# Attention with normalised q and k, then a gated MLP: tokens regrouped from 4 on 112 partitions to 7 on 128, tails packed, and the order of every engine taken from a written plan

## The chip, the cores and the metric

The kernel runs on one core of one Trainium2 chip. The metric is device time in microseconds (us) of one execution; of the kernel before, three runs were timed. TensorE is called PE in the profile (its weight loads PEld), VectorE DVE, ScalarE ACT, GpSimd POOL, SyncE SP. Each engine works through its own list of instructions in order; DMA transfers are issued from the lists of SP, POOL and ACT and land later.

## The reference

Eight batches, 12 heads, 448 tokens, head size 64, all float32. First attention on RMS-normalised q and k, then a gated MLP on the joined heads (768 columns).

```python
q_n, k_n = rmsnorm(q, g_q), rmsnorm(k, g_k)          # x / sqrt(mean(x*x) + 1e-6) * g
scores = matmul(q_n, k_n^T) / 8
attn = exp(scores - max);  attn = attn / (sum(attn) + 1e-9)
x = matmul(attn, v), heads joined                     # (8, 448, 768)
h = relu(x @ w_in);  u, w = h[:, :512], h[:, 512:]
w_n = (w - mean(w)) / sqrt(var(w) + 1e-6)             # over the 512 columns
w_s = w_spatial @ w_n + b_spatial                     # mixes the 448 tokens
out = (u * w_s) @ w_out                               # (8, 448, 768)
```

## The kernel before, in words

**Tiling.** A token index is 4p + c, with p on 112 partitions and c from 0 to 3. So keys come in four tiles of 112, q and k tiles are 112x1024 for a group of four heads, and every product whose rows are tokens uses 112 columns of the array. The 24 groups G (8 batches b times 3) hold heads g, g+3, g+6, g+9 of a batch.

**Attention of a group.** Loads of q and k on SP's queue (L76), squares on POOL (L167), sums of squares on DVE (L173), Ln and Exp on ACT for the reciprocal root (L180, L181), scaling to bf16 on POOL (L189). Both tensors are then transposed, for groups 5 to 23 by a DMA on SP's queue (L211) with a scaling of k on DVE (L222), for groups 0 to 4 on PE (L200) with two evictions on DVE (L205, L206). Four steps n follow: each has four score matmuls with 64 rows (L234, two at a time in the two halves of the array) into four PSUM banks, and one ACT exp over all four banks (L244, 112x1792; in the first 12 steps two exps of 112x896). The next group's steps carry `sums` (L266, 16 matmuls with a ones tile of 32 columns, four at a time beside each other), `recip` (L274, L275: Ln and Exp on ACT), `values` (twice 16 matmuls, L285) and `xt_store` (L293, DVE).

**MLP of a batch.** `unit_v` (L311: four token tiles, six matmuls of 512 columns each), relu, `stats` (L317, L318), `ln_rstd` (L325, L326), `ln_apply` (L331, DVE); `unit_u` (L340: four times six matmuls of 448); `unit_s` (L350: the spatial product, four times four of 448, the bias as a 113th row; its gate L353 on DVE); `unit_o` (L364: eight times four of 384; evictions L367 on ACT or L369 on DVE) and the output DMA on SP (L371, L373).

**Order.** The loop over t (four steps a group) writes the order of all engines by hand. Step t computes scores and exps of its group, the sums or values of the group before, and one slice of the MLP of the batch that lies 15 steps back: the first `unit_v` comes at t = 15, after group 3 has all its scores. The last batch's MLP follows the loop. POOL's queue issues v (L80, one DMA a batch), w_in (L135), w_spatial (L140), w_out (L143) and the bias (L144, onto 17 partitions); at t = 15 DVE casts the bias into w_spT (L507), ahead of everything else that DVE has to do there, and DVE copies four transposed tiles of w_spatial after it (L149, L153).

**PSUM.** Four banks hold scores (one tile `pss` of four banks from step 12 on, two of two banks before), four rotate among all other products.

Of the kernel before, what the change touches and what calls it, by code (L numbers as in the profile page):

```python
# [14 lines left out]
PSUM = bass.MemoryType.PSUM  # L15


@with_exitstack
def kernel(
# [13 lines left out]
    nc = tc.nc  # L33
# [3 lines left out]
    P = 112  # L37
    NC = 4
    NG = 3
    scale = 1.0 / math.sqrt(D)  # L40

    pe, act, dve, pool, sync = nc.tensor, nc.scalar, nc.vector, nc.gpsimd, nc.sync

    ctx.enter_context(tc.manual_schedule())

    const = ctx.enter_context(tc.tile_pool(name="const", bufs=1))
    early_pools = ctx.enter_context(ExitStack())
    first = ctx.enter_context(tc.tile_pool(name="first", bufs=1))
    early_qt = ctx.enter_context(tc.tile_pool(name="early_qt", bufs=2))
    ps_e = early_pools.enter_context(tc.tile_pool(name="ps_e", bufs=2, space=PSUM, side="right"))  # L50
    ps_w = ctx.enter_context(tc.tile_pool(name="ps_w", bufs=4, space=PSUM))
    qk_pool = ctx.enter_context(tc.tile_pool(name="qk", bufs=4))
    sq_pool = ctx.enter_context(tc.tile_pool(name="sq", bufs=2))
    qn_pool = ctx.enter_context(tc.tile_pool(name="qn", bufs=2))
    qt_pool = ctx.enter_context(tc.tile_pool(name="qt", bufs=3))
    st_pool = ctx.enter_context(tc.tile_pool(name="st", bufs=4))
    v_pool = ctx.enter_context(tc.tile_pool(name="vp", bufs=2))
    e_pool = ctx.enter_context(tc.tile_pool(name="ep", bufs=4))
    r_pool = ctx.enter_context(tc.tile_pool(name="rp", bufs=2))
    x_pool = ctx.enter_context(tc.tile_pool(name="xp", bufs=2))  # L60
    m_pool = ctx.enter_context(tc.tile_pool(name="mp", bufs=1))
    o_pool = ctx.enter_context(tc.tile_pool(name="op", bufs=3))


    q_g = [q[b].rearrange("(l g) (p c) d -> g p l (c d)", g=NG, c=NC) for b in range(B)]
    k_g = [k[b].rearrange("(l g) (p c) d -> g p l (c d)", g=NG, c=NC) for b in range(B)]
    raw, vb = {}, {}

    def load(G, i, l0=0, nl=4):
        b, g = divmod(G, NG)  # L70
        if nl == 4:
            t = qk_pool.tile([P, 4, NC * D], FP, name="qf" if i == 0 else "kf")
        else:
            t = first.tile([P, 2, NC * D], FP, name=f"f{i}{l0}")
        raw[G, i, l0] = t
        sync.dma_start(out=t, in_=(q_g, k_g)[i][b][g][:, l0:l0 + nl])  # L76

    def load_v(b):
        t = v_pool.tile([P, H, NC, D], BF, name="vt")
        pool.dma_start(  # L80
            out=t.rearrange("p h c d -> p h (c d)"),
            in_=v[b].rearrange("h (p c) d -> p h (c d)", c=NC))
        vb[b] = t

    g_row = const.tile([1, 2, 2, D], FP)
# [3 lines left out]
    for l in (0, 2):  # L89
        load(0, 0, l, 2)  # L90
        load(0, 1, l, 2)
    for G in (1, 2, 3):
        load(G, 0)
        load(G, 1)


    eps = const.tile([128, 1], FP)
    dve.memset(eps, 1e-6)
    one_f = const.tile([1, 1], FP)
    dve.memset(one_f, 1.0)  # L100
    ones = const.tile([P, 32], BF)
    dve.memset(ones, 1.0)
    ident = const.tile([128, 128], BF)
    make_identity(nc, ident)


    w_in_u = const.tile([128, 6, DH], BF)
    w_in_v = const.tile([128, 6, DH], BF)
    w_out = const.tile([128, 4, DM], BF)
    w_spT = const.tile([113, NC, NC, P], BF)  # L110
    w_sp = const.tile([P, NC, S], BF)
    bst = const.tile([113, S], FP)
    vn_t = [const.tile([113, NC, DH], BF, name=f"vn{i}") for i in range(2)]
    for t in vn_t:
        pool.memset(t[96:113, :, :], 1.0)

    ps_d = ps_w.tile([128, 512], FP, name="ps")

    def dummies(n):
        for _ in range(n):  # L120
            pe.matmul(out=ps_d[:, 0:128], lhsT=ident, rhs=ident, start=True, stop=True)

    dummies(50)
    g2_row = const.tile([1, 128], FP)
    g2_col = const.tile([128, 1], FP)
    dve.scalar_tensor_tensor(out=g2_row, in0=g_row[:, 0].rearrange("o t d -> o (t d)"), scalar=scale,
                             in1=g_row[:, 1].rearrange("o t d -> o (t d)"),
                             op0=ALU.mult, op1=ALU.mult)
    ps_g = ps_w.tile([128, 512], FP, name="ps")
    pe.matmul(out=ps_g[:, 0:1], lhsT=g2_row, rhs=one_f, start=True, stop=True)  # L130

    def load_w_in(h):
        w = w_in_v if h else w_in_u
        for l in range(4):
            pool.dma_start(  # L135
                out=w[32 * l:32 * l + 32, :, :],
                in_=moe_w_in[192 * l:192 * l + 192, DH * h:DH * h + DH].rearrange("(j p) f -> p j f", p=32))

    def load_w_sp():
        pool.dma_start(out=w_sp, in_=moe_w_spatial.rearrange("(p c) s -> p c s", c=NC))  # L140

    def load_w_out():
        pool.dma_start(out=w_out, in_=moe_w_out.rearrange("(c p) m -> p c m", p=128))  # L143
        pool.dma_start(out=bst[96:113, :], in_=moe_b_spatial.partition_broadcast(17))  # L144

    def w_sp_unit(sc):
        ps = ps_w.tile([128, 8, 128], BF, name="ps")
        for t in range(NC):
            pe.matmul(out=ps[0:P, t, 0:P],  # L149
                      lhsT=w_sp[:, t, :].rearrange("p (s c) -> p c s", c=NC)[:, sc, :],  # L150
                      rhs=ident[0:P, 0:P], is_transpose=True,
                      start=(t == 0), stop=(t == NC - 1))
        dve.tensor_copy(out=w_spT[0:P, sc, :, :], in_=ps[0:P, 0:NC, 0:P])  # L153


    sqt, sqs, rst, nrm, qkt = {}, {}, {}, {}, {}

    def squares(G, i, l0=0, nl=4, eng=None):
        if nl == 4:
            t = sq_pool.tile([P, 4, NC * D], FP, name="sqt")  # L160
        else:
            t = first.tile([P, nl, NC * D], FP, name=f"s{i}{l0}")
        x = raw[G, i, l0]
        if eng is act:
            act.activation(out=t, in_=x, func=AF.Square, bias=0.0, scale=1.0)
        else:
            (eng or pool).tensor_tensor(out=t, in0=x, in1=x, op=ALU.mult)  # L167
        sqt[G, i, l0] = t

    def reduce(G, i, l0=0, nl=4):  # L170
        if (G, l0) not in sqs:
            sqs[G, l0] = st_pool.tile([P, 2, 4 * nl], FP, name="ms")
        dve.tensor_reduce(out=sqs[G, l0][:, i, :],  # L173
                          in_=sqt.pop((G, i, l0)).rearrange("p l (c d) -> p (l c) d", d=D),
                          axis=AX.X, op=ALU.add)

    def rstd(G, l0=0, nl=4):
        ln = st_pool.tile([P, 2, 4 * nl], FP, name="lnms")
        rst[G, l0] = st_pool.tile([P, 2, 4 * nl], FP, name="rs")
        act.activation(out=ln, in_=sqs[G, l0], func=AF.Ln, bias=eps[0:P, :], scale=1.0 / D)  # L180
        act.activation(out=rst[G, l0], in_=ln, func=AF.Exp, bias=0.0, scale=-0.5)  # L181

    def scaled(G, i, l0=0, nl=4, eng=None):
        if nl == 4:
            t = qn_pool.tile([P, NC, nl, D], BF, name=f"n{i}")
        else:
            t = first.tile([P, NC, nl, D], BF, name=f"n{i}{l0}")
        nrm[G, i, l0] = t
        (eng or pool).tensor_tensor(  # L189
            out=t.rearrange("p c l d -> p l c d"),  # L190
            in0=raw[G, i, l0].rearrange("p l (c d) -> p l c d", d=D),
            in1=rst[G, l0][:, i, :].rearrange("p (l c) -> p l c", c=NC).to_broadcast([P, nl, NC, D]),
            op=ALU.mult)

    def transposes(G, pr):
        ps = ps_w.tile([128, 8, 128], BF, name="ps")
        for i in range(2):
            for c in range(NC):
                x = nrm[G, i, 2 * pr] if (G, i, 2) in nrm else nrm[G, i, 0][:, :, 2 * pr:2 * pr + 2, :]
                pe.matmul(out=ps[:, 4 * i + c, 0:P], lhsT=x[:, c, :, :],  # L200
                          rhs=ident[0:P, 0:P], is_transpose=True,
                          start=(i == 0 and c == 0), stop=(i == 1 and c == NC - 1))
        qT = early_qt.tile([128, NC, P], BF, name=f"qe{pr}")
        kT = early_qt.tile([128, NC, P], BF, name=f"ke{pr}")
        dve.tensor_copy(out=qT, in_=ps[:, 0:4, 0:P])  # L205
        dve.tensor_scalar(out=kT, in0=ps[:, 4:8, 0:P], scalar1=g2_col, scalar2=None, op0=ALU.mult)  # L206
# [404 lines left out]
```

## Time and profile before

| | |
|---|---|
| timed runs | 337.10, 337.59 (median), 338.27 us |
| profiled execution | span 335.8 us from first to last instruction (the profile shows no other time of it) |
| busy | PE 298.2, PEld 144.9, DVE 222.2, ACT 223.5, POOL 187.5 us |
| exps | 84 of 112x1792 at 1662 ns, 24 of 112x896 at 913 ns |
| PE's records | 2484 matmuls |
| DMA | 50.45 MB, mean 150 GB/s |
| granted PE clock | mean 0.937 |

A row of groups reads: line, engine, operation, output and inputs with shapes, count, then busy time and mean length of one, then the engine's idle time just ahead of these instructions and what ended it. A busy PE row runs to the modelled end of a matmul and so overlaps the next one: rates of PE are read from start to start. In the table of windows, PEclk is the granted clock as a share of the full one.

### The profile page before, as it was taken

What the parts mean: (1) busy time and instruction counts of PE and PEld (TensorE: products, weight loads), DVE (VectorE), ACT (ScalarE), POOL (GpSimd) and SP (SyncE); (2) the same over time, 40 slices, a digit from 0 to 9 for tenths busy, and PEclk for the clock granted to TensorE, in tenths of its full rate; (3) what the DMA queues carried; (4) which work ended last, traced back from release to release, by engine and by line L of the source; (5) the groups of instructions that cost most, each with busy time, mean ns of one, the idle gap of its engine ahead of it and who ended that gap; (6) DMA issues with size and microseconds to landing.
All of it is one profiled execution on the core that took longest, in us unless ns stands there. A gap on an engine that the chain in (4) does not pass through costs nothing.

```text
span 335.8 us, 6167 instructions
## 1 busy us (share of the span) xinstructions
PE 298.2 (89%) x2484; PEld 144.9 (43%) x2484; DVE 222.2 (66%) x364; ACT 223.5 (67%) x275; POOL 187.5 (56%) x114
## 2 busy tenths in 40 slices
PE   6757674789999989998999899989998999999993
PEld 6432231434444435443454344434543354435552
DVE  3667754566964977497757877588658964735551
ACT  4648495047877687778687768777877877784331
POOL 5824699747468648665956774795487454000000
PEclk9678595659999999999999999999999999999999
DMA  7993969928458994799389966895679254002205
GB/s 187 241 238 73 187 148 208 207 37 154 111 133 206 190 212 86 206 203 238 68 209 191 183 155 193 174 208 145 171 191 197 49 129 119 27 2 82 84 0 167
DMA packets 75061, 50.45 MB, mean 150 GB/s; under 512 B 36911, under 2 KB 71440, under 8 KB 75032
## 3 DMA queue, kind: packets, MB, share of 16 engines
q1 hardware_dynamic: 61792, 41.76, 53.9%
q0 software_dynamic: 13232, 8.30, 17.9%
q8 instruction: 19, 0.31, 0.4%
q14 instruction: 10, 0.08, 0.1%
q10 hardware_dynamic: 8, 0.00, 0.0%
HBM read 38.58 MB, written 11.01 MB: 148 GB/s over the span
## 4 chain that ended last, share of the span: by engine, by line
POOL 33%; issue 28%; PE 22%; DVE 6%; DMA 6%; ACT 3%; ACTq 0%; POOLq 0%; DVEq 0%; SPq 0%
POOL sqt L167 19%; POOL n L189 11%; PE ps L311 4%; DMA bst<-in_moe_b_spatial_dram 4%; PE ps L364 3%; PE ps L340 3%; PE ps L285 2%; PE pss L234 2%; PE ps L266 2%; ACT et L244 2%; PE ps L350 2%; POOL vt L80 2%; DVE n L189 1%; PE pse L234 1%; PE ps L200 1%
## 5 line engine op out<-in xcount | busy, mean ns | idle before, releaser
L244 ACT ACTIVATE et<-pss 112x1792 bf16<-112x1792 f32 x84 | 139.6, 1662 | 58.4 <-PE pss L234 57.5
L189 POOL TENSOR_TENSOR n<-qf,rs 112x1024 bf16<-112x1024 f32 x22 | 45.9, 2086 | 88.2 <-ACT rs L181 76.4
L173 DVE TENSOR_REDUCE ms<-sqt 112x16 f32<-112x1024 f32 x46 | 55.6, 1215 | 45.2 <-POOL sqt L167 45.2
L364 PE MATMUL ps<-w_out,gt 128*112 128x384 bf16 x256 | 47.6, 330 | 2.9 <-DVE osb L369 2.6
L234 PE MATMUL pss<-qT,kT 64*112 64x448 bf16 x304 | 44.5, 369 | 5.8 <-ACT et L244 5.2
L311 PE MATMUL ps<-w_in_v,xt 128*112 128x512 bf16 x192 | 49.3, 404 | 0.0
L285 PE MATMUL ps<-et,vt 112*32 112x448 bf16 x768 | 46.1, 361 | 0.0
L167 POOL TENSOR_TENSOR sqt<-qf 112x1024 f32<-112x1024 f32 x22 | 42.6, 1934 | 0.0
L167 POOL TENSOR_TENSOR sqt<-kf 112x1024 f32<-112x1024 f32 x22 | 41.7, 1895 | 1.3 <-DMA kf<-in_k_dram 1.2
L340 PE MATMUL ps<-xt,w_in_u 128*128 128x448 bf16 x192 | 40.1, 354 | 0.0
L364 PEld LDWEIGHTS <-gt 128*112 128x112 bf16 x256 | 31.2, 129 | 19.9 <-issue 12.5
L293 DVE TENSOR_TENSOR xt<-ps,rc 128x448 bf16<-128x448 f32 x48 | 29.3, 615 | 15.5 <-PE ps L285 15.5
L189 POOL TENSOR_TENSOR n<-kf,rs 112x1024 bf16<-112x1024 f32 x19 | 38.8, 2040 | 0.0
L311 PEld LDWEIGHTS <-xt 128*112 128x112 bf16 x192 | 24.6, 137 | 21.1 <-issue 9.5
L369 DVE COPY osb<-ps 112x384 f32<-112x384 f32 x46 | 24.4, 552 | 7.6 <-PE ps L364 5.1
L234 PEld LDWEIGHTS <-kT 64*112 64x112 bf16 x304 | 14.9, 124 | 31.7 <-issue 31.4
L285 PEld LDWEIGHTS <-vt 112*32 112x32 bf16 x768 | 16.3, 97 | 25.4 <-issue 17.1
L350 PE MATMUL ps<-w_spT,vn 112*128 112x448 bf16 (+1 forms) x128 | 26.9, 353 | 0.0
L244 ACT ACTIVATE et<-pse 112x896 bf16<-112x896 f32 x24 | 20.5, 913 | 9.6 <-PE pse L234 9.5
L340 PEld LDWEIGHTS <-w_in_u 128*128 128x128 bf16 x192 | 17.1, 98 | 20.9 <-issue 7.2
L266 PE MATMUL ps<-et,ones 112*32 112x448 bf16 x384 | 24.8, 382 | 0.0
L317 DVE BATCH_NORM_STATS2 s<-vs 112x6 f32<-112x512 bf16 x32 | 21.7, 680 | 2.5 <-ACT vs L301 2.5
(59 smaller groups left out, 276.0 us busy)
## 6 DMA issues: line engine op xcount, KB each, us to landing
out_dram<-osb SPq DMA_DIRECT2D x31, 336.0 KB, 3.0
qf<-in_q_dram SPq DMA_DIRECT2D x23, 448.0 KB, 8.1
kf<-in_k_dram SPq DMA_DIRECT2D x23, 448.0 KB, 7.3
vt<-in_v_dram POOLq DMA_DIRECT2D x8, 672.0 KB, 13.1
w_in_v<-in_moe_w_in_dram POOLq DMA_DIRECT2D x4, 192.0 KB, 5.8
w_in_u<-in_moe_w_in_dram POOLq DMA_DIRECT2D x4, 192.0 KB, 8.0
w_out<-in_moe_w_out_dram POOLq DMA_DIRECT2D x1, 768.0 KB, 13.4
f<-in_q_dram SPq DMA_DIRECT2D x2, 224.0 KB, 4.0
```

The source lines that it names most:

```text
L167: (eng or pool).tensor_tensor(out=t, in0=x, in1=x, op=ALU.mult)
L173: dve.tensor_reduce(out=sqs[G, l0][:, i, :], in_=sqt.pop((G, i, l0)).rearrange("p l (c d) -> p (l c) d", d=D), axis=AX.X, op=ALU.add)
L189: (eng or pool).tensor_tensor(out=t.rearrange("p c l d -> p l c d"), in0=raw[G, i, l0].rearrange("p l (c d) -> p l c d", d=D), in1=rst[G, ...
L234: pe.matmul(out=ps[:, h, 0:S], lhsT=kT[64 * h:64 * h + 64, 2 * (n % 2) + c, :], rhs=qT[64 * h:64 * h + 64, :, :], start=True, stop=True)
L244: act.activation(out=exps[G, n // 2][:, c0:c0 + m, :], in_=ps[:, 0:m, 0:S], func=AF.Exp, bias=0.0, scale=1.0)
L266: pe.matmul(out=ps[32 * l:32 * l + 32, 0:S], lhsT=ones, rhs=exps[G, l // 2][:, 2 * c + l % 2, :], start=(c == 0), stop=(c == NC - 1), tile ...
L285: pe.matmul(out=ps[32 * l:32 * l + 32, 0:S], lhsT=vb[b][:, 3 * l + g, c, 32 * half:32 * half + 32], rhs=exps[G, l // 2][:, 2 * c + l % 2, ...
L293: dve.tensor_tensor(out=xts[b][:, 2 * g + half, :], in0=pst.pop((G, half))[:, 0:S], in1=rec[G], op=ALU.mult)
L311: pe.matmul(out=ps[0:P, :], lhsT=xts[b][:, j, c * P:(c + 1) * P], rhs=w_in_v[:, j, :], start=(j == 0), stop=(j == 5))
L340: pe.matmul(out=ps[:, 0:S], lhsT=w_in_u[:, j, 128 * f:128 * f + 128], rhs=xts[b][:, j, :], start=(j == 0), stop=(j == 5))
L350: pe.matmul(out=ps[:, 0:S], lhsT=vn_t[b % 2][0:kp, c, 128 * f:128 * f + 128], rhs=w_spT[0:kp, c, :, :].rearrange("p c s -> p (c s)"), star ...
L364: pe.matmul(out=ps[0:P, 0:384], lhsT=gts[b][:, f, c * P:(c + 1) * P], rhs=w_out[:, f, r], start=(f == 0), stop=(f == 3))
```

## The change

The kernel body is rewritten; the arithmetic of the reference stays. What differs:

- **Seven tokens a partition.** A token is 7p + c with p on 64 partitions, and two heads share the 128 partitions. A q or k tile of a group is 128x896 (rows of 1792 bytes), one DMA each.
- **128-key score tiles.** A head's keys are three tiles of 128 and a tail of 64. Twelve score matmuls of a group have 64 rows and 128 columns (units 0 to 5, two each); unit 6 is four matmuls of 64x64, two heads' tails beside each other in one bank. Each unit has one exp of 128x896: seven a group, 168 in all.
- **Sums and values** are passes of four matmuls (words s, a, b, four passes each); the tail pass uses ones and v with zeros on the other head's 64 rows (vz, zeroed once).
- **Transposes.** k of groups 1 to 23 and q of three of them go through PE (7 matmuls of 128 columns, word P, 26 times; group 0 in halves, word p) with one eviction of 128x896 (K: 22 on DVE, 4 on ACT); q of the other 20 groups goes by DMA (T).
- **MLP tiles.** Token tiles are three of 128 and a tail of 64. Word W puts the v product's tail of batch b (6 matmuls of 512, 64 columns at column 0 of the array) beside the output product's tail of batch b-1 (8 matmuls of 384, 64 columns at column 64). `ln_apply` moves to ACT (word A, Identity with scale and bias from tiles; one small DVE product w makes the bias).
- **Who does what.** Squares: 31 on POOL, 13 on ACT, 2 on DVE; scalings: 40 on POOL, 6 on DVE. v comes in four DMAs a batch on POOL's queue (32 in all, runs of 384 and 128 bytes); the bias comes in one row on SP's queue, its cast is a single row.
- **PSUM** is one tile of eight banks, each use with bank numbers from the plan; scores take any two banks, read as `ps[:, a:b+1:b-a, :]`.
- **Order.** The loop over t is gone. A string of 1649 words gives the order; a word's engine list is served in the order of the words. U and V come in three passes of two matmuls, sums and values in four, so that other work can stand between.

```diff
+PLAN = """
+l.1.0/0 setup//v l.0.0/1 l.1.1 l.0.1 L.1.0/2 L.1.1/3 L.2.1/4 gA//v L.4.0/5 gB/0 z.44/7 L.2.0/6 q.1.0/0/a r.1.0//v
...
+S.4.6/02 s.3.0/7 N.6.1/1/g E.4.6/d/a s.4.0/5 S.5.0/34 y.2//v s.4.1 L.10.1/2 I.7//a s.3.1 y.1//v s.4.2 J.7//a L.9.0/6
...
+SLOTS = dict(raw=7, sqt=3, nrm=4, qT=4, kr=0, kT=4, et=18, rc=2, vs=2, vn=2, us=2, os=4)
...
+    ps = psp.tile([128, 8, 512], FP, name="ps")
...
+    def op_wb(sl, e):
+        sync.dma_start(out=bst[64:65, :], in_=moe_b_spatial.rearrange("(o s) -> o s", o=1))
...
+    def op_P(sl, e, G, i):
+        where["tp", G, i] = sl[0]
+        p_ = ps[:, sl[0], :].bitcast(BF)
+        n = nrm[where.pop(("n", G, i))]
+        for m in range(C):
+            c = order[m] if i else m
+            pe.matmul(out=p_[:, 128 * m:128 * m + 128], lhsT=n[:, c, :, :], rhs=ident,
+                      is_transpose=True, start=(m == 0), stop=(m == C - 1))
...
+    def op_S(sl, e, G, u):
+        where["S", G, u] = sl
+        qT, kT = qTs[where["qk", G, 0]], kTs[where["qk", G, 1]]
+        if u == 6:
+            todo = [(r, hh, 6, T, 64 * hh, r) for hh in range(2) for r in range(2)]
+        else:
+            heads, j = unit(G, u)
+            todo = [(r, hh, 2 * j, 2 * T, 0, n) for n, (r, hh) in enumerate(heads)]
...
+            pe.matmul(out=ps[at:at + w, sl[n], 0:S],
+                      lhsT=kT[64 * r:64 * r + 64, hh, :, :].rearrange("q c p -> q (c p)")[:, 64 * c:64 * c + w],
+                      rhs=qT[64 * r:64 * r + 64, :, 64 * hh:64 * hh + 64],
+                      start=True, stop=True, tile_position=(64 * r, at))
+
+    def op_E(sl, e, G, u):
+        a, b = where.pop(("S", G, u))
+        where["et", G, u] = sl[0]
+        act.activation(out=ets[sl[0]], in_=ps[:, a:b + 1:b - a, 0:S], func=AF.Exp, bias=0.0, scale=1.0)
...
+    def op_W(sl, e, b):
...
+                todo.append((j / 6, dict(out=ps[0:64, sl[0], :], lhsT=xts[b % 2][:, j, TAIL:], rhs=w_in[:, j, DH:],
+                                         start=(j == 0), stop=(j == 5), tile_position=(0, 0))))
...
+                todo.append(((n + 0.5) / 8, dict(
+                    out=ps[64:128, sl[h - 2], 0:384], lhsT=gts[(b - 1) % 2][:, f, TAIL:],
+                    rhs=w_out[:, f, 384 * h:384 * h + 384], start=(f == 0), stop=(f == 3),
+                    tile_position=(0, 64))))
+        for _, args in sorted(todo, key=lambda x: x[0]):
+            pe.matmul(**args)
...
+    def op_A(sl, e, b, m):
...
+            act.activation(out=y, in_=x, func=AF.Identity, bias=nbs[b % 2][rows, m:m + 1], scale=rvs[b % 2][rows, m:m + 1])
...
+    for word in PLAN.split():
+        name, sl, e = (word.split("/") + ["", ""])[:3]
+        name, *args = name.split(".")
+        here["op_" + name]([int(x, 36) for x in sl], e, *map(int, args))
```

In a word such as `S.4.1/24` or `E.4.1/5/a` the part ahead of the first slash is the operation with its group (or batch) and unit, then come the banks or buffers, then the engine (a ACT, v DVE, g POOL).

## The prediction

> **What bounds the kernel now.** I read the page first, then the table of windows, then PE and the chain of waits inside the windows.
>
> ```profile
> span 335.8 us, 6167 instructions
> PE 298.2 (89%) x2484; PEld 144.9 (43%) x2484; DVE 222.2 (66%) x364; ACT 223.5 (67%) x275; POOL 187.5 (56%) x114
> PE   6757674789999989998999899989998999999993
> ACT  4648495047877687778687768777877877784331
> PEclk9678595659999999999999999999999999999999
> ```
>
> PE is the fullest engine, and its row has two parts: a quarter of the span at 5 to 7 tenths with the clock often near half, then 9 to the end. The windows put numbers to that:
>
> ```profile
> core 0: us, PE busy (x) PEld busy (x) DVE busy (x) ACT busy (x) POOL busy (x), PEclk, DMA share, GB/s
> 12.00:30.00 18.00, 13.80 (x114) 7.47 (x112) 11.41 (x12) 11.83 (x18) 6.73 (x4) 0.67 1.04 210
> 51.00:66.00 15.00, 9.38 (x48) 4.46 (x48) 7.63 (x8) 4.08 (x5) 13.57 (x10) 0.54 1.21 208
> 75.00:306.00 231.00, 222.62 (x1912) 103.39 (x1914) 165.18 (x276) 174.45 (x201) 139.71 (x76) 1.00 0.73 151
> ```
>
> From 75 on PE is busy 96% at the full clock; ACT and DVE have a quarter of the time free. That part is bound by PE. The start is not: ACT's rows in order of time show one hole, and the chain of waits says who made it.
>
> ```profile
> 69.58 1.66 ACT L244 ACTIVATE et<-pss 112x1792 bf16<-112x1792 f32 x1 [11.98 <-PE pss L234]
> ```
>
> ```profile
> 52.67 12.84 DMA bst<-in_moe_b_spatial_dram
> 65.53 0.56 DVE w_spT L507
> ...
> 68.54 0.99 PE pss L234 x4
> ```
>
> The bias, last in POOL's queue, lands after 12.84 us; the cast of it stands at the head of DVE's list, k's eviction is behind it, PE's scores wait for k, ACT for the scores. The first v product of the MLP (L311) starts at 71.7.
>
> **What a product costs on PE.** From PE's own rows, start to start:
>
> ```profile
> 289.18 0.94 PE L285 MATMUL ps<-et,vt 112*32 112x448 bf16 x16
> 290.05 1.31 PE L340 MATMUL ps<-xt,w_in_u 128*128 128x448 bf16 x6
> 291.29 0.58 PE L234 MATMUL pss<-qT,kT 64*112 64x448 bf16 x4
> 291.81 2.44 PE L340 MATMUL ps<-xt,w_in_u 128*128 128x448 bf16 x12
> 294.19 0.59 PE L234 MATMUL pss<-qT,kT 64*112 64x448 bf16 x4
> ```
>
> Twelve matmuls of 448 take 2.38 us, six 1.24: 0.19 each, and 0.10 that belongs to the run, not to a matmul. The 16 of L285 are four rounds of four beside each other: 0.87 = 4 x 0.19 + 0.11. The four of L234 are two rounds: 0.52 = 2 x 0.19 + 0.14. The same subtraction for L311 (x12 2.73, x6 1.43) gives 0.216 and 0.13, for L364 (x12 2.09, x8 1.44) 0.162 and 0.14. A run's fixed part comes at each change between score, 32-column and full-array matmuls; it is 0.13 to 0.14 where weights have 112 columns, 0.10 where 128, and weight loads differ too:
>
> ```profile
> L311 PEld LDWEIGHTS <-xt 128*112 128x112 bf16 x192 | 24.6, 137 | 21.1 <-issue 9.5
> L340 PEld LDWEIGHTS <-w_in_u 128*128 128x128 bf16 x192 | 17.1, 98 | 20.9 <-issue 7.2
> ```
>
> **PE, before and after, at the full clock.** Before: v products 192 x 0.216 = 41.5; u 192 x 0.189 = 36.3; spatial 128 x 0.189 = 24.2; output 256 x 0.162 = 41.5; scores 192 pairs x 0.189 = 36.3; sums and values (384 + 768)/4 x 0.189 = 54.4; transposes 5.4; 262 changes of shape x 0.125 = 32.8; dummies 4.3. Sum 276.7. After, counted in the plan's words: V 72 x 0.432 = 31.1; U 36.3; H 24.2; O 48 x 0.648 = 31.1; W about 12 (the two tails side by side: 6 x 0.216 = 1.30 beside 8 x 0.162 = 1.30; one after the other it would be 2.6); scores 168 rounds x 0.189 = 31.8; sums and values 288 x 0.189 = 54.4; 210 transposing matmuls of k and q 11 (0.053 each, from eight 128-column dummies in 0.85 us at the half clock); the w_spatial transposes about 1.5; 219 changes x 0.105 = 23.0; dummies 5.1. Sum 261.6, so **15 us less**: tails -8.7, score tiles -4.5, changes of shape -9.8, transposes +7. Bounds of what no row shows: W between 1.30 and 2.6 each (0 to +11 in all; I take side by side, as L285's four are); the 64x64 unit one or two rounds (0 to +4.5, likewise); k's moving rows in 64-column pieces as L234's 112-column pieces (0).
>
> The Trainium skill speaks against such interleaving: "TensorEngine Tiling (Array Packing)", section Tiling Modes, says that changing the tiling mode drains the array. The rows agree in kind, with their 0.10 to 0.14. By the rule alone a plan that cuts U and V in three and sums in four should lose; the counted changes fall, since sums and values of one or two groups stand together.
>
> **The other engines.** ACT: 168 exps x 913 = 153.4 (before 160.1); recip 27; Ln and Exp of the norms 12.7; `ln_apply` 32 x about 0.76 = 24 (nearest rows: the relu of 512 at 597, and Ln with a bias tile 312 against Exp without 229); squares 13 x 0.94 = 12.2; relus and output evictions 24.5; the rest 12. Sum about 266 against 223.5, so ACT becomes nearly as full as PE. But lengths overlap: two exps in a row take 1.72, not 1.83, and the rows at 16.55 (x4, 3.32) give 0.81 each, so in a row ACT needs about 230 to 235. DVE loses `ln_apply` (13.6) and 1/8 of L173's 55.6, gains evictions of 128x896 (about 0.82, as L222's 811): about 215, hidden at 70%. POOL falls from 187 to about 155 in spite of 32 v issues in place of 8 (w_in's issues of like size 0.58): hidden. SP: 20 transposes of 1.22 in place of 38, 56 output issues in place of 33: lighter. DMA: no more bytes, q and k rows of 1792 in place of 1024 bytes, half of the transposes gone, v in smaller runs: its share of 0.73 should not rise. Had any of these no cover, it is DVE that is next after ACT.
>
> Identity is in no row of before. The rows show Copy, Relu, Square, Ln and Exp under a single table load (L88, 1283 ns). If Identity needed its own table, A's 20 runs on ACT would cost 20 x 2 x 1.28 = 51; I take 0 by the five functions that share one load. "ScalarE: Activation LUTs", section "Table sets: the hidden batching unit", names identity among the cheap functions in every set; by it the cost is 0 as well, but no run here shows it yet.
>
> **The start.** The bias now comes on SP's queue and its cast stands after the first MLP products, so the hole of 12 goes. What is late next is ACT: the plan has 26 exps ahead of the first v product. First exp at about 12.5 (before 11.80; ACT's list ahead of it sums to 6.3). Then 26 x 0.81 to 0.913 = 21 to 24, and recip, norms, one square and one eviction 7.4: 41 with no wait. Loads by then: six groups 5.5 MB, w_in 3.1, v 1.4 = 10 MB; at the 208 GB/s of the rows above 48, but a part of w_in may land after. I take **46**, between 42 (no wait) and 57.6 (where before ended the exps of its 16th step, just ahead of the hole, so nothing gained but the hole).
>
> **The sum.** PE's list from the first v product on is 235.5, of which 34 after the last exp. At 95.6% busy (before: 33.6 of each 35.15 us of a batch) the first 201 take 210.6, the last at 98.5% 34.7. Span = 46 + 245.3 + 5.6 (before: last matmul at 330.2, end at 335.8: eviction, output DMA, landing) = 296.9. The median of the runs lies 1.8 over the profiled span: **299**.
>
> **The rivals.**
> - *Start not shortened beyond the hole* (loads bind): first v product at 57.6, all else the same: 310. For it: DMA share 1.04 and 1.21 in two windows of the start. Against: longer rows, and PE has no need of w_out and w_spatial early.
> - *PE and ACT in lockstep*: until the last exp ACT holds 214 and PE 201, each served in order with eight banks between them; a wait of one is a wait of the other. At 90% in place of 95.6%: 201/0.90 = 223.7, +13: 312; at 87% 320. For it: ACT's idle on L234 is 57.5 us now, harmless with a quarter free. Against: scores of two or three units are queued ahead of their exps in the plan.
> - *Slower*: all of PSUM is one tile, and 128 of the 168 score units sit in banks that are not neighbours. If such an exp is held to read the banks between as well, PE's writes there wait up to one exp, 0.913. From (337.6 - 299)/0.913 = 42 such waits on the change is slower; at half of the 128, 357. For it: nothing in the trace, before had separate tiles. Against: the two strides are plain in the instruction.
> - *No effect*: the PE saving eaten by small waits at all 219 changes: 0.17 each would do it, 337.
>
> **How the numbers follow.** Forecast (288 to 306) 0.54; start not shortened 0.12; lockstep 0.19 (310 to 324); no effect 0.05, of which a third is within 0.3%; slower 0.10. 299 is the likeliest case. The range reaches from 288 (first product at 42, 98.5% busy throughout) to 322 (57.6 or lockstep at 87%, or both tails unpacked plus lockstep at 91%) and leaves out 0.18. A difference of 0.3%, 1 us, is about what a measurement of this kernel can tell from none. Faster 0.88, same 0.02, slower 0.10.
>
> **What would show it.** After: first v product at 42 to 50 with no ACT hole over 3 us ahead of it; a batch period of 30.5 to 31.5 in place of 35.15; fixed part 0.10 at each change; W's 14 matmuls within 1.5 us; exps 0.81 to 0.91; one table load. It is wrong if PE's rows show waits on ACT's exps over some 15 us in the middle, if W takes 2.6, or if PE's clock is half after 60.

## The result: 379.7 us, slower by 12%

The changed kernel takes 379.7 us (median of four runs, 378.94 to 380.45) against 337.72 before (four runs of the same session): ratio 1.124, interval 1.121 to 1.127. The forecast of 299 and its range up to 322 were wrong, in sign too. What came about is the rival that I had called "Slower" and given 0.10.

### The profile after

The page of the changed kernel, with the lines that answer to those shown of before:

```profile
span 377.6 us, 6689 instructions
...
PE 296.3 (78%) x2661; PEld 141.2 (37%) x2661; DVE 209.9 (56%) x340; ACT 248.5 (66%) x383; POOL 151.0 (40%) x123
...
PE   4967878877886976976678797888689686879993
...
ACT  5687858755875886866656777678687444675261
...
PEclk9976999989999899998999899999999799999998
```

No engine is full any more. Before, PE's row went to 9 after a quarter of the span and stayed there; now it lies mostly between 6 and 8 until the last tenth, and ACT's lies no higher. The clock isn't the reason: its row is at 8 or 9 in all but three slices (mean 0.956, before 0.937). The windows, from the first v product of the MLP to the last exp and from there on:

```profile
core 0: us, PE busy (x) PEld busy (x) DVE busy (x) ACT busy (x) POOL busy (x), PEclk, DMA share, GB/s
50.00:337.00 287.00, 225.59 (x2025) 103.47 (x2026) 156.96 (x248) 195.18 (x296) 127.44 (x94) 0.96 0.55 116
337.00:372.00 35.00, 34.40 (x264) 18.28 (x256) 18.78 (x37) 17.17 (x33) 0.00 (x0) 1.00 0.29 78
```

While exps run, PE is busy 225.6 of 287 us, 79%; as soon as there are none left, 98%. So PE is not slow, it waits, and only while ACT has exps to do. The table of waits (engine, line, what ended the wait: us in total, times, longest) says for whom:

```profile
ACT et L514 <- PE ps L506: 22.1, 33, 1.9
...
PE ps L651 <- ACT et L514: 12.9, 17, 1.6
PE ps L506 <- ACT et L514: 12.8, 19, 1.2
...
PE ps L539 <- ACT et L514: 11.8, 15, 1.0
DVE gt L670 <- ACT et L514: 10.5, 7, 2.9
...
PE ps L580 <- ACT et L514: 8.9, 11, 1.1
...
ACT et L514 <- PE ps L651: 8.4, 10, 1.5
...
ACT et L514 <- PE ps L580: 6.0, 8, 1.1
```

PE's u products (L651), v products (L580) and sums and values (L539) wait for exps, and exps wait for them. The u and v products have no data in common with the exps: they neither make scores nor read an exp's output. All that they share is the PSUM tile. (Sums and values do read exps; the banks below tell these waits apart.) PE's longest waits in these rows are 1.0 to 1.6 us; an exp takes 0.915. Rows in order of time show the pattern:

```profile
190.40 1.04 PE L580 MATMUL ps<-w_in,xt 128*128 128x512 bf16 x4
...
191.47 0.92 ACT L514 ACTIVATE et<-ps 128x896 bf16<-128x896 f32 x1 [0.77 <-PE ps L580]
...
192.44 1.02 PE L580 MATMUL ps<-w_in,xt 128*128 128x512 bf16 x4 [1.00 <-ACT et L514]
...
193.07 0.92 ACT L514 ACTIVATE et<-ps 128x896 bf16<-128x896 f32 x1 [0.68 <-PE ps L580]
...
194.04 1.02 PE L580 MATMUL ps<-w_in,xt 128*128 128x512 bf16 x4 [0.57 <-ACT et L514]
```

Counting rows against words gives their banks. The first row is `V.3.0.0/2` and `V.3.2.0/6`, v products into banks 2 and 6. The exp at 191.47 is that of unit `S.13.6/17`, which lies in banks 1 and 7: it waits for the v products, which write neither. The next passes of the two v products wait until it ends. Then comes the exp of `S.13.5/03`, banks 0 and 3, with bank 2 between: it waits for the pass that writes bank 2, and the last passes wait for it. PE and ACT take turns although no bank is used by both.

I matched every PE row and every exp to its word in this way. PE has 73 waits (62.6 us beyond what a change of shape costs) that end 0.02 to 0.09 us after the end of an exp whose two banks enclose the one that PE writes next, and none of these products reads that exp's output; 10 (4.2 us) that end with an exp of the very bank; 42 others of 13.7 us. The other way, 52 exps (43 us) start when a product into a bank between them has ended, and 17 (7.5 us) when their own scores have.

### The profile page after: what moved, and what is told of

It is laid out like the page before. It is cut to its first block, busy times and chain, and to the rows that moved or that the text cites. A ratio compares the mean times of both kernels' runs of the same rounds, so it can differ in the third digit from the quotient of the medians.

```text
span 377.6 us, 6689 instructions
## 1 busy us (share of the span) xinstructions
PE 296.3 (78%) x2661; PEld 141.2 (37%) x2661; DVE 209.9 (56%) x340; ACT 248.5 (66%) x383; POOL 151.0 (40%) x123
## 5 line engine op out<-in xcount | busy, mean ns | idle before, releaser
L514 ACT ACTIVATE et<-ps 128x896 bf16<-128x896 f32 x168 | 148.5, 915 | 75.4 <-PE ps L506 22.1
L404 POOL TENSOR_TENSOR nrm<-raw,rs 128x896 bf16<-128x896 f32 x40 | 67.3, 1690 | 110.8 <-ACT rs L390 50.6
L506 PE MATMUL ps<-qT,kT 64*128 64x448 bf16 (+1 forms) x384 | 56.6, 373 | 13.4 <-ACT et L514 12.8
L361 POOL TENSOR_TENSOR sqt<-raw 128x896 f32<-128x896 f32 (+1 forms) x32 | 52.9, 1658 | 32.8 <-DMA raw<-in_q_dram 18.1
L651 PE MATMUL ps<-xt,w_in 128*128 128x448 bf16 x192 | 50.6, 365 | 12.9 <-ACT et L514 12.9
L372 DVE TENSOR_REDUCE ss<-sqt 128x14 f32<-128x896 f32 x46 | 48.4, 1076 | 2.2 <-ACT sqt L359 1.5
L539 PE MATMUL ps<-et,vt 128*32 128x448 bf16 x576 | 43.8, 373 | 7.1 <-ACT et L514 7.0
L580 PE MATMUL ps<-w_in,xt 128*128 128x512 bf16 x144 | 41.4, 383 | 8.9 <-ACT et L514 8.9
L679 PE MATMUL ps<-w_out,gt 128*128 128x384 bf16 x192 | 39.2, 337 | 6.9 <-DVE xt L564 2.9
L539 PE MATMUL ps<-et,ones 128*32 128x448 bf16 x384 | 33.7, 378 | 3.4 <-ACT et L514 3.3
L506 PEld LDWEIGHTS <-kT 64*128 64x128 bf16 (+1 forms) x384 | 16.0, 98 | 52.6 <-issue 48.8
L651 PEld LDWEIGHTS <-w_in 128*128 128x128 bf16 x192 | 17.6, 99 | 36.1 <-issue 24.0
L539 PEld LDWEIGHTS <-vt 128*32 128x32 bf16 x576 | 16.2, 98 | 23.6 <-issue 16.7
L580 PEld LDWEIGHTS <-xt 128*128 128x128 bf16 x144 | 13.2, 98 | 25.2 <-issue 15.4
```

The source lines that it names most:

```text
L361: eng.tensor_tensor(out=t, in0=x, in1=x, op=ALU.mult)
L372: dve.tensor_reduce(out=sss[G % 3][:, i].rearrange("p r c -> p (r c)"), in_=sqt[where.pop(("sq", G, i))].rearrange("p r (c d) -> p (r c) d ...
L404: engines[e or "g"].tensor_tensor(out=nrm[sl[0]].rearrange("p c r d -> p r c d"), in0=raw[where["raw", G, i]].rearrange("p r (c d) -> p r ...
L506: pe.matmul(out=ps[at:at + w, sl[n], 0:S], lhsT=kT[64 * r:64 * r + 64, hh, :, :].rearrange("q c p -> q (c p)")[:, 64 * c:64 * c + w], rhs= ...
L514: act.activation(out=ets[sl[0]], in_=ps[:, a:b + 1:b - a, 0:S], func=AF.Exp, bias=0.0, scale=1.0)
L539: pe.matmul(out=ps[32 * l:32 * l + 32, bank, 0:S], lhsT=w, rhs=et_of(G, l, j), start=(n == 1), stop=(n == 4), tile_position=(0, 32 * l))
```

## The experiments

Two theories. **A, banks between:** an exp that reads banks a and b through a stride is ordered against every writer of a bank from a to b, both ways. **B, the order itself:** with ACT this full, the plan makes PE and ACT wait for each other whatever the banks (my lockstep rival, far worse than priced). Each timed kernel has four runs (`b1_bias` ten), beside runs of before with medians from 338.41 to 339.22.

**1. The same words, other banks.** 332 banks lie between the two of an exp, summed over the 168 units. `e1_neighbours` renumbers the banks so that every unit has two neighbours (0 between), `e2_far` so that none has (695 between). Words, order and how soon a bank is used again stay.

```diff
 (one changed line of PLAN, of 123 in e1_neighbours and 124 in e2_far: after / e1_neighbours / e2_far)
-... S.4.5/17 c.0.1//v S.4.1/24
+... S.4.5/45 c.0.1//v S.4.1/12
+... S.4.5/16 c.0.1//v S.4.1/07
```

> The changed kernel with the same words in the same order on every engine, but banks renumbered so that the two banks of each of the 168 score units are neighbours (before: 40 of 168); how soon a bank is used again is kept (median 8 words). Theory A (an exp that reads two banks also holds the banks between them, against PE's writes and behind them): the 73 waits of PE that end with such an exp (62.6 us beyond the change of shape) go, and the exps' own waits of that kind; 300 to 318. Theory B (PE and ACT in lockstep, each nearly full and served in order): nothing that B speaks of is changed; 372 to 385.

> The changed kernel with the same words in the same order, banks renumbered the other way: none of the 168 units has neighbours, 695 banks lie between in sum (changed kernel 332). Theory A: the waits grow about as the count of banks between, so some 50 to 80 us on top: 415 to 460. Theory B: 375 to 390.

Measured: `e1_neighbours` 309.31 us (308.36 to 310.33), ratio to before 0.911, interval 0.906 to 0.917. `e2_far` 509.09, ratio 1.502, interval 1.493 to 1.512. The page of `e1_neighbours`, with its group of exps (busy, mean ns, then idle time ahead and what ended most of it):

```profile
span 308.4 us, 6673 instructions
...
PE 282.2 (92%) x2661; PEld 137.9 (45%) x2661; DVE 212.1 (69%) x340; ACT 241.4 (78%) x383; POOL 151.1 (49%) x123
...
PE   3959999995999499999799999999999999999991
...
L514 ACT ACTIVATE et<-ps 128x896 bf16<-128x896 f32 x168 | 145.4, 917 | 16.1 <-PE ps L506 13.6
```

The same group in `e2_far`:

```profile
L514 ACT ACTIVATE et<-ps 128x896 bf16<-128x896 f32 x168 | 153.2, 917 | 191.7 <-PE ps L539 39.0
```

An exp is no slower (917 ns in both, 915 after); what changes is the wait ahead of it: 16.1, then 75.4 with the banks of the change, then 191.7 us. In `e1_neighbours` no wait on a bank between is left, PE's row is back at 9, and exps wait for their own scores, L506. That is A; B holds the order responsible, and the order is the same in all three. A's price by the count was too simple: `e2_far` lies above the 415 to 460 that A gave it. The change pays 70.4 us for 332 banks, 0.21 each; `e2_far` at that rate would be 457 and takes 52 more. Its granted clock is 0.802 in place of 0.956, and PE's 2661 matmuls are busy 358.4 us in place of 296.3, so much of the excess may be the clock; no run separates the two.

**2. The same banks, two reads.** `e3_split` keeps the change's own bank numbers and cuts each exp into two of one bank.

```diff
-        act.activation(out=ets[sl[0]], in_=ps[:, a:b + 1:b - a, 0:S], func=AF.Exp, bias=0.0, scale=1.0)
+        for n, x in enumerate((a, b)):
+            act.activation(out=ets[sl[0]][:, n, :], in_=ps[:, x, 0:S], func=AF.Exp, bias=0.0, scale=1.0)
```

> The changed kernel with its own banks, but each exp of 128x896 over two banks made two exps of 128x448 over one bank each, so that no read has a bank between. ACT gets 168 instructions more, each with a fixed part of some 0.07 to 0.17 (913 for 896 elements, 537 to 577 for 448). Theory A: the false waits go, ACT's load grows by 12 to 28: 305 to 335. Theory B: ACT fuller, so slower: 390 to 405.

Measured: 312.67 us (311.49 to 313.18), ratio 0.922, interval 0.917 to 0.927. Its group of exps:

```profile
L515 ACT ACTIVATE et<-ps 128x448 bf16<-128x448 f32 x336 | 156.3, 563 | 11.8 <-PE ps L506 11.2
```

With twice as many exps and ACT busier by 9 us (250.4 against 241.4) the kernel is 67 us faster than the change. So it isn't the bank numbers as such, it is one read that spans them. Both ways out cost nearly the same, 309.3 and 312.7.

**3. What is left of e1: one small product.** `e1_neighbours` was 10 over the forecast, and its PE row has four dips, one in the start and three behind it. In the first of the three the timeline shows this:

```profile
66.23 5.30 DVE L630 SCALAR_TENSOR_TENSOR nb<-mv,rv 128x4 f32<-128x4 f32 x1
...
66.53 1.70 POOL L404 TENSOR_TENSOR nrm<-raw,rs 128x896 bf16<-128x896 f32 x1
...
68.19 3.31 POOL L361 TENSOR_TENSOR sqt<-raw 128x896 f32<-128x896 f32 x2
...
73.21 1.31 PE L539 MATMUL ps<-et,vt 128*32 128x448 bf16 x12 [4.34 <-DVE xt L564]
```

Word `w`, four elements a partition, takes 5.30 us, until POOL's three products have ended at 71.50; DVE's list stands behind it, and PE waits 4.34 for an eviction in that list. The next `w` takes 4.82 us (102.57), and PE waits 4.21 for `kT`. Of the eight, the four with no POOL product beside them take 0.155 to 0.165, the four others 0.58 to 5.30. The Trainium skill, "SBUF — State Buffer", section "Who interferes with whom", says that a DVE instruction with two inputs from SBUF contends with a GpSimd instruction that reads SBUF, and that one with at most one input does not, outside certain fast modes. Theory **C**: it is the two SBUF inputs; the rival: it is this operation, or its place in the list. `e4_scalars` writes `w` as four instructions with the factor as a per-partition scalar; `e7_two_inputs` keeps two SBUF inputs with another operation; `e6_scalars_only` is `e4_scalars` with the change's own banks.

```diff
 (e4_scalars, against e1_neighbours; e6_scalars_only the same against the change)
-        dve.scalar_tensor_tensor(out=nbs[b % 2], in0=mvs[b % 2][:, :, 0], scalar=-1.0, in1=rvs[b % 2],
-                                 op0=ALU.mult, op1=ALU.mult)
+        for m in range(4):
+            dve.tensor_scalar(out=nbs[b % 2][:, m:m + 1], in0=mvs[b % 2][:, m, 0:1], scalar1=rvs[b % 2][:, m:m + 1],
+                              scalar2=-1.0, op0=ALU.mult, op1=ALU.mult)
 (e7_two_inputs, against e1_neighbours)
+        dve.tensor_tensor(out=nbs[b % 2], in0=mvs[b % 2][:, :, 0], in1=rvs[b % 2], op=ALU.mult)
+        dve.tensor_scalar(out=nbs[b % 2], in0=nbs[b % 2], scalar1=-1.0, scalar2=None, op0=ALU.mult)
```

> e1_neighbours with one edit: the small product of word w (minus mean times reciprocal root, 128x4) is no longer one DVE instruction with two tensors in SBUF as inputs but four with one tensor and a column of scalars. In e1_neighbours that instruction took 0.15 to 5.30 us, and each long one ends within 0.05 us of the end of a row of POOL products; PE then stood idle for 4.5, 4.4 and 1.4 us. Theory: DVE holds such an instruction until POOL pauses. Then the four short ones take some 0.1 each, the holes go, and the clock with them: 296 to 304. Rival: the wait is for something else that DVE's list stands behind (reciprocal roots from ACT, a semaphore), so another instruction takes it over: 307 to 311.

> e1_neighbours with word w as a DVE product of two tensors in SBUF (128x4) and a DVE product with -1 after it: the same inputs as in e1_neighbours under another operation. Theory (an instruction of DVE that reads two tensors from SBUF waits until POOL pauses, whatever the operation): the product takes up to 4 to 5 us as in e1_neighbours, 304 to 311. Rival (only that one operation is slow, or the order of DVE's list was the cause): some 0.2 us each, 293 to 297 as in e4_scalars.

> The changed kernel with its own banks and the one edit of e4_scalars (word w as four DVE instructions with one tensor and scalars). It tells whether the two losses add up. In the changed kernel the two-input form held ACT's next instruction for 9.3 us in all, 3.97 at most. If they add: 379.7 - 15 = 362 to 368. If the waits for banks hide this one (PE waits for an exp either way): 374 to 380.

Measured: `e4_scalars` 294.25 us (293.4 to 294.9), ratio 0.870, interval 0.865 to 0.876, faster than before and after, and a little below the 296 to 304 expected. `e7_two_inputs` 312.71 (311.98 to 314.07), ratio 0.920, interval 0.913 to 0.927: no gain, and a little above the theory's 304 to 311. `e6_scalars_only` 376.26 (372.45 to 376.97), ratio 1.106, interval 1.097 to 1.115, in its rival's range. The rows of the tile `nb` (count; shortest/median/longest ns, first and last start) in `e7_two_inputs`, then in `e4_scalars`:

```profile
L630 DVE TENSOR_TENSOR nb<-mv,rv x8: 154/370/5421, 66.8 to 292.8; 128x4 f32<-128x4 f32 x8
L631 DVE TENSOR_SCALAR nb<-nb x8: 170/170/1611, 72.2 to 293.0; 128x4 f32<-128x4 f32 x8
```

```profile
L631 DVE TENSOR_SCALAR nb<-mv,rv x32: 202/205/216, 65.3 to 273.0; 128x1 f32<-128x1 f32 x32
```

Another operation with two SBUF inputs is held as long (5.42); the 32 instructions with one input and a scalar are never held (longest 0.216), though 12 of them run beside a POOL product. So C for `w`, and the page's rule on two inputs agrees. The trace of before has the hold as well: a scaling on DVE with two SBUF inputs beside squares on POOL, and the same instruction just after.

```profile
16.68 3.53 DVE L189 TENSOR_TENSOR n<-kf,rs 112x1024 bf16<-112x1024 f32 x1 [0.65 <-ACT rs L181]
17.21 1.90 POOL L167 TENSOR_TENSOR sqt<-kf 112x1024 f32<-112x1024 f32 x1
...
20.13 1.21 DVE L189 TENSOR_TENSOR n<-qf,rs 112x1024 bf16<-112x1024 f32 x1
```

3.53 us for work of 1.21: it ends 1.1 us after POOL's product does.

One SBUF input alone is no protection, though. The product with -1 in `e7_two_inputs` (L631, one tensor input) once took 1.611 and ended 0.02 after a POOL product. In the trace of before, k's scaling has one SBUF input and a per-partition scalar:

```profile
L222 DVE TENSOR_SCALAR kT<-kr,g_col x19: 441/445/1836, 78.6 to 289.4; 128x896 bf16<-128x896 bf16 x19
```

Seven of the 19 take 1.10 to 1.84 us, and each of these ends 0.25 after a POOL product beside which it started. The page excepts certain fast modes from its rule for one input; no run here shows in which mode an instruction ran.

PE's rows in `e1_neighbours` show 9.7 us of waits behind DVE's list (4.3, 4.2 and 1.2) that `e4_scalars` hasn't, and the mean clock goes from 0.956 to 0.981; what else makes up the 15.1 us between them no run separates. `e6_scalars_only` shows that the two losses cover each other. Without the bank waits the cure of `w` brings 15.1 us, with them 3.4 (14.3 and 4.9 against the runs of before beside each); with `w` cured the banks cost 82.0, otherwise 70.4.

**4. The best one, and whether PE bounds it.** The page and the windows of `e4_scalars`:

```profile
span 291.6 us, 6683 instructions
...
PE 273.8 (94%) x2645; PEld 135.3 (46%) x2661; DVE 202.3 (69%) x364; ACT 240.9 (83%) x383; POOL 151.1 (52%) x123
...
PE   2968999999999999999999999999999999999991
```

```profile
14.00:44.00 30.00, 25.99 (x293) 11.19 (x292) 24.27 (x28) 27.83 (x41) 17.68 (x18) 0.89 0.87 184
44.00:252.00 208.00, 205.80 (x2024) 98.64 (x2040) 148.85 (x267) 189.65 (x299) 127.69 (x94) 1.00 0.77 161
252.00:285.00 33.00, 32.90 (x245) 17.51 (x240) 19.20 (x42) 16.18 (x32) 0.00 (x0) 1.00 0.29 79
```

First ACT is the fullest (27.83 of 30), then PE, 98.9% and 99.7%. `e5_serial` takes back one part of the change there: W's two tails one after the other. Its recorded expectation names `e1_neighbours` as its base; it was built on `e4_scalars`, and is compared with that here.

```diff
-        for _, args in sorted(todo, key=lambda x: x[0]):
+        for _, args in todo:
```

> e1_neighbours with one edit: in word W the six matmuls of the v product's tail are issued first and the eight of the output product's tail after them, not by turns. In e1_neighbours a W takes 1.165 us from first to last issue. If PE works the list in order and only neighbours in the list run beside each other, a W takes 6 x 0.216 + 8 x 0.162 = 2.6, 1.2 us more, seven times. Theory (PE bounds this kernel once the false waits are gone): 8 us more, 315 to 319. Rival (slack between ACT, DVE and PE hides it): 309 to 312.

Measured: 297.43 us (296.88 to 298.13), ratio to before 0.879, interval 0.874 to 0.884; 3.2 over `e4_scalars`, not the 8 of the theory. W's 14 matmuls take 1.623 us from first to last start in place of 1.165. One after the other they would take 2.4 (6 x 0.216 + 7 x 0.162), so part of the output tail still starts beside the v tail. Seven times 0.458 is 3.2, as much as the medians differ. The four runs of each spread over 1.3 to 1.5 us, and in the two profiled runs the stretch from the first v product to the end of the last matmul differs by 2.6 (241.6 and 244.2). Within that, what PE loses here shows in full in the time: PE bounds this kernel.

**5. My reading of the start.** The prediction put the hole of 12 us in ACT's row of before down to the bias. `b1_bias` is the kernel before with the bias early, on SP's queue.

```diff
+    sync.dma_start(out=bst[96:113, :], in_=moe_b_spatial.partition_broadcast(17))
...
-        pool.dma_start(out=bst[96:113, :], in_=moe_b_spatial.partition_broadcast(17))
```

> The kernel before with one edit: the bias is loaded on SP's queue behind the first q and k loads, not last in POOL's queue. The prediction put the whole hole of 12 us ahead of group 4's exps down to this load. If so: 324 to 328. Rival: PE's list also waits for w_spatial (4.17 us at 60.07) and, at the half clock, for its own work, so that only the part after the last of these is won: 331 to 336.

Measured: 338.54 us (336.76 to 340.63), ratio 0.9995, interval 0.996 to 1.003: nothing is won, and both ranges were wrong. The timeline of `b1_bias`:

```profile
60.23 0.66 PE L149 MATMUL ps<-ident,w_sp 112*112 112x112 bf16 x4 [4.74 <-DMA w_sp<-in_moe_w_spatial_dram]
...
60.69 5.32 PE L311 MATMUL ps<-w_in_v,xt 128*112 128x512 bf16 x12
...
63.17 2.02 DVE L507 CAST w_spT<-bst 17x448 bf16<-17x448 f32 x1
...
68.26 1.66 ACT L244 ACTIVATE et<-pss 112x1792 bf16<-112x1792 f32 x1 [11.06 <-PE pss L234]
```

The hole stays at 11.06. PE's own list waits 4.74 for w_spatial and then does twelve v products at half the clock (0.43 a product) ahead of the scores. The cast of the bias ends at 65.19, before PE goes on from these products (65.81). The bias was the last of several things that end together; the chain names only the last one. These rows correct another number of mine: the first v product of before starts at 60.5, not at 71.7, which was the second lot.

## Why the prediction was wrong, point by point

- **The step that failed** is in the sum: "PE's list from the first v product on is 235.5, of which 34 after the last exp. At 95.6% busy ... the first 201 take 210.6". They took 287.5 (50.2 to 337.6), so 201 of list fill 70% of it; the 79% of the windows counts each matmul to its modelled end. These 77 us are nearly all of the 81 from 299 to 379.7; the other 4 are the first v product, at 50.2 in place of 46. Two waits that the sum put at nothing made the loss.
- **Banks between, 70.4 us** (379.7 to 309.3). I had the mechanism, the 42 waits from which it decides, and 128 of 168 units in the diff, and still gave it 0.10, because the trace of before showed nothing of it. That trace couldn't: there scores have tiles of their own. `e1_neighbours`, `e2_far` and `e3_split` show it. PE had 73 such waits at 0.86, 62.6 us: count and price each close to the rival's (64 at 0.913, giving 357). What the rival missed is that exps wait for the products as well, so that the two engines take turns.
- **Word w, 15.1 us** (309.3 to 294.25), wasn't a term of the sum at all. I wrote that an instruction on DVE is hidden at 70%. A share of busy time hides nothing when one instruction stands for five us with an eviction behind it that PE needs.
- **"PE and ACT in lockstep"**, 0.19 for waits of a full ACT and eight banks, did not happen as such. With both causes gone ACT is busy 91% and PE 98.9% of the middle.
- **The tell-tale** of the prediction, waits of PE on exps over some 15 us in the middle, was the right one: the groups above alone have 46.4 (12.9 + 12.8 + 11.8 + 8.9), those for an exp of the very bank among them.
- **PE's ledger held**, read in `e1_neighbours` from start to start at the full clock: four O matmuls 0.650 (0.648 in the sum), seven transposes 0.391 (0.371), a change of shape 0.096 (0.105), W 1.165 from first to last start and 1.42 to the next product (1.30 and a change, side by side), the 64x64 unit in one round, 0.22 (0.189).
- **The other engines held**: ACT busy 241 without the holds (266 summed, 230 to 235 in a row), `ln_apply` 803 ns (760), DVE 212 (215), POOL 151 (155), one table load with Identity in use. All of that was hidden, as said, but for word `w`.
- **The start nearly held, in part for a wrong reason.** First v product at 50.2 after, 44.75 in `e1_neighbours`, 43.8 in `e4_scalars`, against 46 (42 to 50). ACT is the fullest engine there, as forecast (27.83 of 30 us in `e4_scalars`); that the bias load made the old hole fell with `b1_bias`, and the old first v product, read as 71.7, is at 60.5.
- **The forecast without the two holds**: a span of 296.9 and 299 us; `e4_scalars`, which lacks them, has 291.6 and 294.25. It is 5 ahead: the first v product comes 2.2 earlier, and the 201 us of list up to the last exp take 208.0 in place of 210.6. What the change meant to do is worth 44 us (338.41 to 294.25); its banks and one four-element product cost nearly twice that, 85.5.

**Open.** The profile puts PE's waits down to semaphores that exps release; they go with other bank numbers or other reads, and an exp of two banks takes 915 to 917 ns either way. The Trainium skill, "PSUM — Partial Sum Buffer", section "PSUM bank collisions raise a hardware error", asks for a semaphore guard by bank and quadrant, and by that rule a bank between would need none. No run here shows the strided read without its waits, so whether the chip needs them wasn't tried. Nor is it settled what the last 52 us of `e2_far` are, or in which cases a DVE instruction with one SBUF input is held.

## What to carry to other kernels

When one instruction reads two PSUM banks through a stride, count every bank from the first to the last as taken: give it neighbours, or read each bank by itself (here 309.3 and 312.7 us, against 379.7). Keep DVE instructions with two SBUF inputs out of stretches where POOL runs products back to back, even small ones. A per-partition scalar in place of the second input was the cure here, for one column at a time (0.202 to 0.216); it is no general one, as k's scaling in before shows (up to 1.84). And if a rival's count stands in the diff and only its price is unknown, its chance may not be set by the silence of a trace that could not show it.

## What the runs showed of the hardware

- A DVE product of four elements a partition with two SBUF inputs stood 5.30 us, over three POOL products in a row (1.70 and two in 3.31), not one: DVE did not get in between them. It had started 0.30 before the first of them, while POOL issued a DMA (65.69 to 66.51). Alone it takes 0.155.
- A DVE product with one SBUF input and a per-partition scalar (128x896, bf16) took 0.44 us, and up to 1.84 when it started beside a POOL product; those held ended 0.25 after that product, and the next POOL product didn't hold them further.
- Matmuls that use the other column half of the array start before earlier ones in PE's list: in `e5_serial` the first output product of a W, seventh in the list, starts 0.46 us after the first v product, the sixth v product at 1.10. The 14 took 1.623 from first to last start, not 2.4.
- The mean granted clock was 0.981 in `e4_scalars`, where PE waits least, and 0.802 in `e2_far`, where it waits most, but not in step with the waits: `e1_neighbours` has 0.956 like the change, 70.4 us apart.
- Cutting an exp of two banks in two costs ACT little: 168 exps were 145.4 us busy, 336 of half the size 156.3.
